# A Linformer attention with a gated FFN: PSUM banks of the first batch laid out by hand, two head groups reordered, and the second batch's K projected apart from V

## The chip, the cores and the metric

The kernel runs on one core of a Trainium2 chip. The core has five engines with instruction streams of their own: TensorE (PE, the matmuls), VectorE (DVE), ScalarE (ACT), GpSimd (POOL) and SyncE (SP). Here POOL and SP mostly start DMA transfers. PE writes its results into eight PSUM banks of 128 partitions by 512 fp32 values; ACT and DVE read them there. The metric is the time of one execution on the device, in microseconds; the number given is the median of several runs.

## The reference

Eight batches, eight heads, 1024 positions, 64 values per head. K and V are first projected along the sequence from 1024 rows to 64 (E and F), so that the softmax of each position runs over 64 scores only. The heads are put side by side to rows of 512, and these go through a gated feed-forward layer with 1536 hidden values.

```python
k_proj = np.einsum('ks,bhsd->bhkd', E, k)          # (8, 8, 64, 64)
v_proj = np.einsum('ks,bhsd->bhkd', F, v)
scores = np.matmul(q, k_proj.transpose(0, 1, 3, 2)) / np.sqrt(64)
attn = softmax(scores)                             # over the 64 projected rows
x = np.matmul(attn, v_proj)                        # then to (8 * 1024, 512)
gate = 1.0 / (1.0 + np.exp(-(x @ w_gate)))
out = (gate * (x @ w_val)) @ w_out                 # w_gate, w_val: 512 x 1536, w_out: 1536 x 512
```

## The kernel before

**How the order is made.** Every operation is handed to a planner (`Plan.add`, L38) with the engine, what it reads and writes and the PSUM bank that it uses. Each engine runs its operations in the order in which they were handed over; the planner only adds semaphore waits where an operation depends on one of another engine. A bank is one such resource (`x=[("bank", b)]` in `mm`, `act` and `dve`, L202 to L218): a matmul into a bank waits for whoever read the bank last, and a reader waits for the reader before it, on whatever engine. So an operation that waits holds up all that was handed over to its engine behind it. There is no other scheduling: the order of the calls is the order of the work.

**Banks.** Four banks are called pF0 to pF3 (`FB`), four pA0 to pA3 (`AB`). A `Ring` (L191) gives them out in turn. `whole` (L200) turns over pA0 to pA3 and pF0 to pF2, `ffn` over the four F banks, `att` over the four A banks. Each call of `next()` takes the next one, whether it is free or not.

**First batch (L951 to L998).** All data come from HBM, so the start is a chain: E and F are transposed (`project_consts`, L413); `project` (L447) multiplies K's four heads by E; `keep_k` copies the product out, `turn_k` (L487) transposes it back on PE, and ACT writes `kpD`. In `half_unit` (L513) come, for one half of each position block and one group R of four heads: `qt` (PE transposes Q, two engines copy it to `qT`), `sc` (scores, then exponentials to `eT` on ACT), `den` (sums of the exponentials; DVE makes the reciprocal `rden` and splits it into two bf16 parts, `rhi` and `rhl`), `bc` (PE spreads the reciprocals over the partitions, ACT copies them to `rb`), and `xo` (attention times V; DVE multiplies by `rb` into `xT`). V is projected by `v_part` (L972) and copied to `vpD` by `keep_v` on ACT and DVE. `busy(n)` (L437) puts n matmuls of the identity by itself into pF3, whose result nobody reads. `first_pair` (L877) then begins the feed-forward layer with two of its column blocks at once, with `xo` of the second head group in between.

**The main loop (L1007 to L1060).** For each batch b it makes a list `todo` of steps: two halves (blk) of 12 steps `mstep` (L870: four matmuls for the gate, four for the value, 128x512 each, then `gate`: the sigmoid as a tanh on ACT to `sig`, and the product on DVE to `hT`), and output projections `oproj` (L923: 12 matmuls, a copy on DVE, a DMA by SP) in between. The step uses two F banks, so that step m + 2 needs the banks of step m. `put(i, fn)` hangs a piece of the attention of the next batch behind entry i of the list; `spots` (L1038, L1040) holds these places. For the first batch the entries are 0 to 10 (first half; entry 0 is the pair of the steps 0 and 1), 11 to 22 (steps 0 to 11 of the second half) and 23 to 26 (four `oproj`).

**The second batch's attention** (`attention(1)`, L666) differs from the later ones. `kv` (L669) projects K and V into one bank, 32 matmuls, and copies K once and V four times, all on ACT; `turn_kd` transposes K on PE; `den` makes four reciprocals, `split` the bf16 parts; `bc` spreads by matmuls. Batches from the third on use DMA transposes and POOL for these steps. `sc` and `xo` take four banks of `att` each.

POOL issues all loads in program order: those of the first batch, of Q(1), K(1), V(1) and w_out (which waits for the transposes of Q(1)), then of the batches after. K(1) lies in buffer KV2, which V(2) is loaded into later. SP issues the DMA transposes of Q(1), four transfers, and the stores.

Of the kernel before, what the change touches and what calls it, by code (L numbers as in the profile page):

```python
# [8 lines left out]
BF16 = mybir.dt.bfloat16  # L9
# [109 lines left out]
def bass_linformer_attn__then__ffn_glu_sigmoid_kernel(  # L119
# [18 lines left out]
    with contextlib.ExitStack() as es:  # L138
# [58 lines left out]
                self.turn += 1  # L197
                return b

        whole, ffn, att = Ring(AB + FB[:3]), Ring(FB), Ring(AB)  # L200

        def mm(b, o, lhsT, rhs, r, start=True, stop=True, tp=None, tr=False):  # L202
            kw = {}
# [8 lines left out]
        def act(o, i, r, w, b=None, func=AF.Copy, scale=1.0):  # L212
            x = [] if b is None else [("bank", b)]
            return add("ACT", lambda e: e.activation(o, i, func, scale=scale), r=r, w=w, x=x)  # L214

        def dve(fn, r, w, b=None):
            x = [] if b is None else [("bank", b)]
            return add("DVE", fn, r=r, w=w, x=x)  # L218
# [294 lines left out]
        def half_unit(hf, ring):  # L513
# [2 lines left out]
            qv = qT[s][:, :, :].rearrange("p (R x) c -> p R x c", R=2)  # L516

            def qt(R, engines):
                bk = ring.next()
                ob = bank[bk][:, :].bitcast(BF16)  # L520
                for x in range(4):
                    for t in range(2):
                        c = x * 2 + t
                        mm(
                            bk,
                            ob[:, c * P : (c + 1) * P],
                            Qb[s][:, 4 * R + x, (2 * hf + t) * P : (2 * hf + t + 1) * P],
                            ident[:, :],
                            [("Q", s, hf, R), "ident"],
                            tr=True,  # L530
                        )
                o = qv[:, R, :, 256 * hf : 256 * hf + 256]
                i = ob[:, :].rearrange("p (x c) -> p x c", x=4)
                for rr, eng in enumerate(engines):
                    oo, ii = (a[:, 2 * rr : 2 * rr + 2, :] for a in (o, i))
                    ws = [("qT", s, hf, R, rr)]
                    if eng == "ACT":
                        act(oo, ii, [], ws, b=bk)
                    else:
                        dve(lambda e, oo=oo, ii=ii: e.tensor_copy(oo, ii), [], ws, b=bk)  # L540

            def sc(R):
                bks = [ring.next(), ring.next()]
# [122 lines left out]
        def attention(b):  # L666
            s = b % 2

            def kv():  # L669
                bk = att.next()  # L670
                if b == 1:
                    project(2 * b % 3, 0, [bk, bk], 0)
                    project((2 * b + 1) % 3, 1, [bk, bk], 256)
                    keep_k(bk, 0)
                    keep_v([bk, bk], 256, ["ACT"] * 4)
                    return
                for t in range(NT):
                    for w in range(2):
                        n = (2 * b + w) % 3
                        src = KV[n][:, :, :].rearrange("p h (t d) -> p t h d", t=NT)  # L680
                        mm(
                            bk,
                            bank[bk][64 * w : 64 * w + 64, :],
                            EFT[:, t, 64 * w : 64 * w + 64],
                            src[:, t, :, :],
                            [("KV", n, 0), ("KV", n, 1), ("EFT", t // 4)],
                            start=(t == 0),
                            stop=(t == NT - 1),
                            tp=(0, 64 * w),
                        )  # L690
                act(
                    kpd[:, :, :, :],
                    bank[bk][0:64, :]
                    .rearrange("p (h d) -> p h d", h=H)
                    .unsqueeze(2)
                    .to_broadcast([64, H, 2, DH]),
                    [],
                    ["kpd"],
                    b=bk,
                )  # L700
                for g in range(2):
                    act(
                        vpD[64 * g : 64 * g + 64, :, :].rearrange("p h d -> p (h d)"),
                        bank[bk][64:128, :],
                        [],
                        [("vpD", h, g, R) for h in range(2) for R in range(2)],
                        b=bk,
                    )

            def turn_kd():  # L710
                if b == 1:
                    turn_k(att)
                    return
                add(
                    "SP",
                    lambda e: e.dma_start_transpose(
                        kpD[:, :, :],
                        kpd[:, :, :, :].rearrange("p h g d -> p (h g d)"),
                    ),
                    r=["kpd"],  # L720
                    w=[("kpD", 0), ("kpD", 1)],
                    dma="kpD",
                )
# [98 lines left out]
            def xo(r2):  # L822
                for r in (2 * r2, 2 * r2 + 1):
# [13 lines left out]
                    for g in range(2):  # L837
# [10 lines left out]
                            b=bks[g],  # L848
                        )

            return [
                kv,
                turn_kd,
                lambda: sc(0),
                lambda: sc(1),
                den,
                split if b == 1 else gather,
                (lambda: bc(0)) if b == 1 else (lambda: spread(0)),
                (lambda: bc(1)) if b == 1 else (lambda: spread(1)),
                lambda: xo(0),  # L860
                lambda: xo(1),
            ]
# [88 lines left out]
        start_loads()  # L951
        constants()
        project_consts()
        busy(40)
        qt, sc, den, bc, xo = half_unit(0, whole)
        for R in range(2):
            bk = whole.next()
            project(0, 0, [bk, bk], 0, R)
            busy(4)
            keep_k(bk, 0, R)  # L960
            turn_k(whole, R)
            busy(8)
        qt(0, ("DVE", "ACT"))
        busy(6)
        sc(0)
        qt(1, ("DVE", "DVE"))
        busy(6)
        den(0)
        sc(1)
        busy(4)  # L970

        def v_part(R, ring):  # L972
            bks = [ring.next(), ring.next()]
            project(1, 1, bks, 0, R)
            keep_v(bks, 0, ["ACT", "DVE", "ACT", "DVE"], R)

        bc(0)
        den(1)
        v_part(0, whole)
        busy(4)  # L980
        bc(1)
        xo(0)
        busy(8)
        for _ in range(-att.turn % 4):
            att.next()
        v_part(1, att)
        start_xo = half_unit(0, att)[4]
        load_q(1)
        load_k(1)
        load_v(1)  # L990
# [16 lines left out]
        for b in range(B):  # L1007
            todo = []
            for blk in (2 * b, 2 * b + 1):
                ms = [[m] for m in range(NF)]  # L1010
                if blk == 0:
                    ms = [[0, 1]] + ms[2:]
                if blk == 1:
                    gaps = {11: [0, 1, 2, 3]}
                else:
                    gaps = {2: [0], 5: [1], 8: [2], 11: [3]}
                for m in ms:
                    if len(m) == 2:
                        todo.append(lambda: first_pair(lambda: start_xo(1)))
                    else:  # L1020
                        todo.append(lambda blk=blk, m=m[0]: mstep(blk, m))
                    if blk >= 1:
                        for tt in gaps.get(m[-1], ()):
                            todo.append(lambda blk=blk, tt=tt: oproj(blk - 1, tt, ffn.next()))
            at = {}

            def put(i, fn):
                at.setdefault(i, []).append(fn)

            if b == 0:  # L1030
                qt, sc, den, bc, xo = half_unit(1, att)
                put(5, lambda: (qt(0, ("DVE", "ACT")), qt(1, ("DVE", "ACT"))))
                put(6, lambda: sc(0))
                put(7, lambda: (den(0), sc(1)))
                put(8, lambda: (den(1), bc(0)))
                put(9, lambda: (xo(0), bc(1)))
                put(10, lambda: xo(1))
                spots = (16, 17, 18, 19, 20, 20, 22, 23, 24, 25)  # L1038
            else:
                spots = (3, 6, 10, 13, 16, 16, 20, 23, 26, 29)  # L1040
            if b + 1 < B:
                for i, fn in zip(spots, attention(b + 1)):
                    put(i, fn)
            def load_next(n):
                load_k(n)
                load_q(n)
                load_v(n)

            if b == 0:
                put(17, lambda: load_next(2))  # L1050
                put(25, lambda: transpose_q(2))
            else:
                if b + 2 < B:
                    put(4, lambda b=b: load_next(b + 2))
                    put(20, lambda b=b: transpose_q(b + 2))
            for i, slot in enumerate(todo):
                slot()
                for fn in at.get(i, ()):
                    fn()
            assert max(at, default=0) < len(todo)  # L1060
        last = 2 * B - 1
        for tt in range(4):
            oproj(last, tt, whole.next())

        plan.emit(nc, es, final=[f"out{i}" for i in range(4)])

# [27 lines left out]
```

The softmax here doesn't subtract the row's maximum and nothing guards it: scores larger than these inputs give would overflow.

## Time and profile before

| what | value | where from |
|---|---|---|
| median of 3 runs | 576.91 us (576.17 to 576.95) | the runs |
| the profiled execution | 575.25 us | its own time |
| its span | 573.4 us | the profile |
| PE standing, 10.97 to 20.00 us | 9.03 - 7.25 = 1.78 us | busy time by stretches |
| PE standing, 20.00 to 28.80 us | 8.80 - 5.91 = 2.89 us | the same |
| PE standing, 28.80 to 53.70 us | 24.90 - 23.72 = 1.18 us | the same |
| PE standing, 69.60 to 80.46 us | 10.86 - 9.05 = 1.81 us | the same |
| PE standing, 80.46 to 559.70 us | 0.00 us | the same |
| granted PE clock | 1.00 in every stretch | the same |

The span is the time from the first to the last instruction of the profiled execution; that execution's own time is 1.85 us longer, and the median of the other runs 1.66 us longer again. Times inside the execution are counted from the span's start. A line of the timeline holds the start, the duration from the first to the last of a merged group, the engine, the line of the kernel, the operation with output and input, the number of instructions, and in square brackets how long the engine had been idle and what ended it. "PEld" is the loading of weights, which overlaps the matmuls.

When transfers of the first two batches were issued and landed (issue + time to landing, from the answers on the tiles):

| load | issued | landed |
|---|---|---|
| K(0), first and second half of the heads | 1.34, 2.24 | 9.3, 12.0 |
| Q(0), first and second half of the heads | 2.98, 3.73 | 13.4, 14.7 |
| V(0), first and second half of the heads | 4.44, 5.2 | 18.4, 20.9 |
| w_gate and w_val, chunk 3 (steps 6 and 7) | 13.34, 14.07 | 33.0, 34.3 |
| K(1), V(1) | 18.6, 19.5 | 50.1, 56.7 |

### The profile page before, as it was taken

The numbers are of one execution on the slowest core, as the hardware profiler recorded it, in microseconds if no ns is written. First come the engines' busy times: TensorE is split into PE (matmuls) and PEld (weight loads), VectorE is DVE, ScalarE is ACT, GpSimd is POOL, SyncE is SP. The second block draws the span as 40 slices with busy tenths as digits, with TensorE's granted clock in tenths as the row PEclk, the third lists the DMA queues.
The fourth block names the chain that finished last, engine by engine and source line by source line (L and its number), as shares of the span: only waits on it lengthen the run. The fifth ranks groups of instructions, "written<-read, shape, count | busy, mean of one in ns | idle before, by whom it ended". The sixth has DMA issues, their size and how long they took to land.

```text
span 573.4 us, 7766 instructions
## 1 busy us (share of the span) xinstructions
PE 556.9 (97%) x3060; PEld 248.8 (43%) x3060; DVE 251.5 (44%) x403; ACT 176.2 (31%) x310; POOL 107.2 (19%) x148
## 2 busy tenths in 40 slices
PE   5799989999999999999999999999999999999997
PEld 5443434444444444444444444444444444444443
DVE  3546356325633546335453264434463354633332
ACT  2444561342224322333223422144223332222220
POOL 9400200104400071001800035000610007000000
PEclk9999999999999999999999999999999999999999
DMA  9999896955656159430796046670501101010012
GB/s 159 199 201 186 144 204 159 173 112 104 113 117 102 37 113 153 86 84 22 123 170 116 23 85 107 138 105 37 113 19 46 38 20 39 37 38 21 35 38 91
DMA packets 76421, 56.02 MB, mean 98 GB/s; under 512 B 34688, under 2 KB 67968, under 8 KB 76384
## 3 DMA queue, kind: packets, MB, share of 16 engines
q0 software_dynamic: 33984, 29.89, 34.4%
q1 hardware_dynamic: 42400, 25.63, 17.6%
q8 instruction: 24, 0.39, 0.3%
q14 instruction: 13, 0.11, 0.1%
HBM read 60.29 MB, written 16.78 MB: 134 GB/s over the span
## 4 chain that ended last, share of the span: by engine, by line
PE 95%; DVE 3%; ACT 1%; issue 0%; DVEq 0%
PE pF L210 86%; PE pA L210 9%; ACT eT L214 1%; DVE rden L769 1%; DVE xT L639 0%; DVE rden L583 0%; DVE count L327 0%; DVE hT L910 0%; DVE dsel L388 0%; ACT sig L214 0%; DVE rhl L780 0%; DVE rhl L594 0%; DVE ost L937 0%; ACT qT L214 0%; ACT kp L214 0%
## 5 line engine op out<-in xcount | busy, mean ns | idle before, releaser
L910 DVE SCALAR_TENSOR_TENSOR hT<-sig,pF 128x512 bf16<-128x512 f32 x192 | 130.7, 685 | 200.5 <-PE pF L210 153.1
L214 ACT ACTIVATE sig<-pF 128x512 f32<-128x512 f32 x192 | 114.3, 599 | 317.6 <-PE pF L210 315.2
L210 PE MATMUL pF<-xT,wG 128*128 128x512 bf16 x768 | 198.3, 379 | 1.8 <-DVE xT L639 1.8
L210 PE MATMUL pF<-xT,wV 128*128 128x512 bf16 x768 | 197.7, 379 | 0.0
L210 PE MATMUL pF<-wO,hT 128*128 128x512 bf16 x732 | 168.1, 379 | 0.0
L210 PEld LDWEIGHTS pF<-xT,wV 128*128 128x128 bf16 x768 | 75.2, 98 | 90.3
L210 PEld LDWEIGHTS pF<-xT,wG 128*128 128x128 bf16 x768 | 72.2, 98 | 96.6 <-issue 12.9
L815 POOL PARTITION_BROADCAST rb<-rrow x96 | 70.7, 798 | 217.1 <-DMA rrow<-rden 212.0
L210 PEld LDWEIGHTS pF<-wO,hT 128*128 128x128 bf16 x732 | 70.4, 98 | 88.7 <-issue 6.2
L937 DVE TENSOR_SCALAR ost<-pF 128x512 f32<-128x512 f32 x61 | 42.2, 692 | 97.8 <-PE pF L210 95.5
L214 ACT ACTIVATE eT<-pA 128x512 bf16<-128x512 f32 x62 | 32.2, 606 | 9.5 <-PE pA L210 9.5
L840 DVE TENSOR_TENSOR xT<-pA,rb 128x512 bf16<-128x512 f32 x56 | 34.7, 682 | 0.0
L228 POOL DMA_DIRECT2D KV<-in_v_dram x9 | 7.8, 871 | 87.3 <-PE pF L210 84.9
L769 DVE RECIPROCAL rden<-pA 128x128 f32<-128x128 f32 x28 | 23.7, 909 | 0.0
L210 PE MATMUL pA<-KV,EFT 128*64 128x512 bf16 (+2 forms) x176 | 15.4, 319 | 1.0 <-DVE xT L639 1.0
L214 ACT ACTIVATE kpd<-pA 64x1024 bf16<-64x1024 f32 x6 | 6.1, 1017 | 28.3 <-PE pA L210 28.3
L228 POOL DMA_DIRECT2D KV<-in_k_dram x9 | 8.0, 890 | 33.3 <-PE pF L210 33.2
L210 PEld LDWEIGHTS pA<-KV,EFT 128*64 128x64 bf16 x176 | 8.0, 109 | 8.0 <-issue 4.1
L210 PE MATMUL pA<-qT,kpD 64*64 64x512 bf16 (+1 forms) x136 | 10.2, 370 | 0.5 <-ACT qT L214 0.3
L210 PE MATMUL pA<-eT,vpD 64*64 64x512 bf16 (+1 forms) x140 | 10.4, 367 | 0.0
L214 ACT ACTIVATE vpD<-pA 64x512 bf16<-64x512 f32 (+2 forms) x20 | 9.7, 484 | 2.2 <-PE pA L210 1.8
L228 POOL DMA_DIRECT2D Qb<-in_q_dram x11 | 9.4, 866 | 0.0
(70 smaller groups left out, 109.3 us busy)
## 6 DMA issues: line engine op xcount, KB each, us to landing
out_dram<-ost SPq DMA_DIRECT2D x64, 256.0 KB, 2.0
Qb<-in_q_dram POOLq DMA_DIRECT2D x7, 1024.0 KB, 15.9
KV<-in_k_dram POOLq DMA_DIRECT2D x7, 1024.0 KB, 10.8
KV<-in_v_dram POOLq DMA_DIRECT2D x7, 1024.0 KB, 11.4
wO<-in_moe_w_out_dram POOLq DMA_DIRECT2D x1, 1536.0 KB, 13.0
wG<-in_moe_w_gate_dram POOLq DMA_DIRECT2D x5, 256.0 KB, 19.7
wV<-in_moe_w_val_dram POOLq DMA_DIRECT2D x5, 256.0 KB, 20.2
KV<-in_k_dram POOLq DMA_DIRECT2D x2, 512.0 KB, 8.9
```

The costliest lines, as they stand in the source:

```text
L210: return add("PE", lambda e: e.matmul(o, lhsT, rhs, **kw), r=r, x=[("bank", b)])
L214: return add("ACT", lambda e: e.activation(o, i, func, scale=scale), r=r, w=w, x=x)
L228: add("POOL", lambda e: e.dma_start(o, i), r=r, w=w, dma=sem)
L769: lambda e, cc=cc: e.reciprocal(rden[:, cc], bank[bk][:, cc]),
L815: lambda e, n=n, i=2 * rnd + c, j=j, parts=parts: e.partition_broadcast(rb[0:parts, n, :], rrow[32 * j : 32 * j + 1, i, :], channels=parts),
L840: lambda e, r=r, g=g, n=n, bk=bks[g]: e.tensor_tensor(xT[s][:, r, :, 256 * g : 256 * g + 256], bank[bk][:, :].rearrange("p (f c) -> p f c" ...
L910: lambda e: e.scalar_tensor_tensor(hT[blk % 2][:, m, :], sg[:, :], 1.0, bank[pv][:, :], ALU.add, ALU.mult,),
L937: lambda e: e.tensor_scalar(o[:, :], bank[pb][:, :], 0.5, None, op0=ALU.mult),
```

## The change

- `whole` becomes a list of 28 banks in an order written by hand, one entry for each bank that the first half of the first batch takes; `v_part(1)` and the `xo(1)` in `first_pair`, which took banks of `att`, now take them from it, and the last four `oproj` take F banks.
- `qt` takes a bank for each of its two copies, with four transposes each, where one bank held all eight; this holds for both halves of the first batch. In the list, the two banks of `qt(1)` are the same one, pA3.
- In the first half, `sc(1)` goes ahead of `den(0)`, and `den(1)` ahead of `bc(0)`. The fillers change from 40 to 20 at the start, from 8 to 10 behind the first K projection and to 4 behind the second, and by some more from `sc(1)` on.
- For the second batch, `kv` is split into `k_alone` and `v_alone`, each with a bank of `att`. The spots become 13 (K), 14 (its transposes), 16 (V and `sc(0)`), 17 (`sc(1)`), 18 (`den` and `split`), 21 and 23 (`bc`), 24 and 25 (`xo`); they were 16 (K and V), 17, 18, 19, 20 (`den` and `split`), 22, 23, 24, 25.

```diff
--- before.py
+++ after.py
@@ -197,7 +197,24 @@
                 self.turn += 1
                 return b
 
-        whole, ffn, att = Ring(AB + FB[:3]), Ring(FB), Ring(AB)
+        A0, A1, A2, A3 = AB
+        F0, F1, F2, F3 = FB
+        whole = Ring(
+            (A0, A1)
+            + (A2, A3, F0, F1)
+            + (A0, A1)
+            + (F2, A2)
+            + (A3, A3)
+            + (F0, F1)
+            + (A0, A1)
+            + (A2, A0)
+            + (A3, F0)
+            + (F1, F2)
+            + (A1, A2)
+            + (A3, A0)
+            + (A1, A2)
+        )
+        ffn, att = Ring(FB), Ring(AB)
 
         def mm(b, o, lhsT, rhs, r, start=True, stop=True, tp=None, tr=False):
             kw = {}
@@ -516,28 +533,27 @@
             qv = qT[s][:, :, :].rearrange("p (R x) c -> p R x c", R=2)
 
             def qt(R, engines):
-                bk = ring.next()
-                ob = bank[bk][:, :].bitcast(BF16)
-                for x in range(4):
-                    for t in range(2):
-                        c = x * 2 + t
-                        mm(
-                            bk,
-                            ob[:, c * P : (c + 1) * P],
-                            Qb[s][:, 4 * R + x, (2 * hf + t) * P : (2 * hf + t + 1) * P],
-                            ident[:, :],
-                            [("Q", s, hf, R), "ident"],
-                            tr=True,
-                        )
-                o = qv[:, R, :, 256 * hf : 256 * hf + 256]
-                i = ob[:, :].rearrange("p (x c) -> p x c", x=4)
                 for rr, eng in enumerate(engines):
-                    oo, ii = (a[:, 2 * rr : 2 * rr + 2, :] for a in (o, i))
+                    bk = ring.next()
+                    ob = bank[bk][:, :].bitcast(BF16)
+                    for x in range(2):
+                        for t in range(2):
+                            c = x * 2 + t
+                            mm(
+                                bk,
+                                ob[:, c * P : (c + 1) * P],
+                                Qb[s][:, 4 * R + 2 * rr + x, (2 * hf + t) * P : (2 * hf + t + 1) * P],
+                                ident[:, :],
+                                [("Q", s, hf, R), "ident"],
+                                tr=True,
+                            )
+                    o = qv[:, R, 2 * rr : 2 * rr + 2, 256 * hf : 256 * hf + 256]
+                    i = ob[:, 0:512].rearrange("p (x c) -> p x c", x=2)
                     ws = [("qT", s, hf, R, rr)]
                     if eng == "ACT":
-                        act(oo, ii, [], ws, b=bk)
+                        act(o, i, [], ws, b=bk)
                     else:
-                        dve(lambda e, oo=oo, ii=ii: e.tensor_copy(oo, ii), [], ws, b=bk)
+                        dve(lambda e, o=o, i=i: e.tensor_copy(o, i), [], ws, b=bk)
 
             def sc(R):
                 bks = [ring.next(), ring.next()]
@@ -668,12 +684,6 @@
 
             def kv():
                 bk = att.next()
-                if b == 1:
-                    project(2 * b % 3, 0, [bk, bk], 0)
-                    project((2 * b + 1) % 3, 1, [bk, bk], 256)
-                    keep_k(bk, 0)
-                    keep_v([bk, bk], 256, ["ACT"] * 4)
-                    return
                 for t in range(NT):
                     for w in range(2):
                         n = (2 * b + w) % 3
@@ -707,10 +717,17 @@
                         b=bk,
                     )
 
+            def k_alone():
+                bk = att.next()
+                project(2 * b % 3, 0, [bk, bk], 0)
+                keep_k(bk, 0)
+
+            def v_alone():
+                bk = att.next()
+                project((2 * b + 1) % 3, 1, [bk, bk], 0)
+                keep_v([bk, bk], 0, ["ACT"] * 4)
+
             def turn_kd():
-                if b == 1:
-                    turn_k(att)
-                    return
                 add(
                     "SP",
                     lambda e: e.dma_start_transpose(
@@ -848,15 +865,29 @@
                             b=bks[g],
                         )
 
+            if b == 1:
+                return [
+                    k_alone,
+                    lambda: turn_k(att),
+                    v_alone,
+                    lambda: sc(0),
+                    lambda: sc(1),
+                    den,
+                    split,
+                    lambda: bc(0),
+                    lambda: bc(1),
+                    lambda: xo(0),
+                    lambda: xo(1),
+                ]
             return [
                 kv,
                 turn_kd,
                 lambda: sc(0),
                 lambda: sc(1),
                 den,
-                split if b == 1 else gather,
-                (lambda: bc(0)) if b == 1 else (lambda: spread(0)),
-                (lambda: bc(1)) if b == 1 else (lambda: spread(1)),
+                gather,
+                lambda: spread(0),
+                lambda: spread(1),
                 lambda: xo(0),
                 lambda: xo(1),
             ]
@@ -951,7 +982,7 @@
         start_loads()
         constants()
         project_consts()
-        busy(40)
+        busy(20)
         qt, sc, den, bc, xo = half_unit(0, whole)
         for R in range(2):
             bk = whole.next()
@@ -959,32 +990,30 @@
             busy(4)
             keep_k(bk, 0, R)
             turn_k(whole, R)
-            busy(8)
+            busy(10 if R == 0 else 4)
+
+        def v_part(R):
+            bks = [whole.next(), whole.next()]
+            project(1, 1, bks, 0, R)
+            return lambda: keep_v(bks, 0, ["ACT", "DVE", "ACT", "DVE"], R)
+
         qt(0, ("DVE", "ACT"))
         busy(6)
         sc(0)
         qt(1, ("DVE", "DVE"))
         busy(6)
+        sc(1)
         den(0)
-        sc(1)
-        busy(4)
-
-        def v_part(R, ring):
-            bks = [ring.next(), ring.next()]
-            project(1, 1, bks, 0, R)
-            keep_v(bks, 0, ["ACT", "DVE", "ACT", "DVE"], R)
-
+        busy(10)
+        den(1)
         bc(0)
-        den(1)
-        v_part(0, whole)
-        busy(4)
+        v_part(0)()
+        busy(6)
         bc(1)
         xo(0)
-        busy(8)
-        for _ in range(-att.turn % 4):
-            att.next()
-        v_part(1, att)
-        start_xo = half_unit(0, att)[4]
+        busy(4)
+        keep = v_part(1)
+        keep()
         load_q(1)
         load_k(1)
         load_v(1)
@@ -1016,7 +1045,7 @@
                     gaps = {2: [0], 5: [1], 8: [2], 11: [3]}
                 for m in ms:
                     if len(m) == 2:
-                        todo.append(lambda: first_pair(lambda: start_xo(1)))
+                        todo.append(lambda: first_pair(lambda: xo(1)))
                     else:
                         todo.append(lambda blk=blk, m=m[0]: mstep(blk, m))
                     if blk >= 1:
@@ -1028,14 +1057,14 @@
                 at.setdefault(i, []).append(fn)
 
             if b == 0:
-                qt, sc, den, bc, xo = half_unit(1, att)
-                put(5, lambda: (qt(0, ("DVE", "ACT")), qt(1, ("DVE", "ACT"))))
-                put(6, lambda: sc(0))
-                put(7, lambda: (den(0), sc(1)))
-                put(8, lambda: (den(1), bc(0)))
-                put(9, lambda: (xo(0), bc(1)))
-                put(10, lambda: xo(1))
-                spots = (16, 17, 18, 19, 20, 20, 22, 23, 24, 25)
+                qt2, sc2, den2, bc2, xo2 = half_unit(1, att)
+                put(5, lambda: (qt2(0, ("DVE", "ACT")), qt2(1, ("DVE", "ACT"))))
+                put(6, lambda: sc2(0))
+                put(7, lambda: (den2(0), sc2(1)))
+                put(8, lambda: (den2(1), bc2(0)))
+                put(9, lambda: (xo2(0), bc2(1)))
+                put(10, lambda: xo2(1))
+                spots = (13, 14, 16, 16, 17, 18, 18, 21, 23, 24, 25)
             else:
                 spots = (3, 6, 10, 13, 16, 16, 20, 23, 26, 29)
             if b + 1 < B:
@@ -1060,7 +1089,7 @@
             assert max(at, default=0) < len(todo)
         last = 2 * B - 1
         for tt in range(4):
-            oproj(last, tt, whole.next())
+            oproj(last, tt, ffn.next())
 
         plan.emit(nc, es, final=[f"out{i}" for i in range(4)])
```

## The prediction

> **What bounds the kernel now.** I read the busy shares first: TensorE (PE) is busy for 97% of the span, so a change pays only where PE stands still, and costs where it makes PE stand still. The chain of waits says where. From 93 us to 559.7 us it is PE alone, piece after piece as below; no edit to the first two batches is worth anything in there.
>
> ```profile
> PE 556.9 (97%) x3060; PEld 248.8 (43%) x3060; DVE 251.5 (44%) x403; ACT 176.2 (31%) x310; POOL 107.2 (19%) x148
> ```
> ```profile
> 28.82 10.52 PE pF L210 x48
> ...
> 170.12 13.06 PE pF L210 x60
> ```
>
> The table by stretches gives PE's standing time: 1.78 us in 10.97 to 20.00, 2.89 us in 20.00 to 28.80, 1.18 us in 28.80 to 53.70, 1.81 us in 69.60 to 80.46, nothing between 80.46 and 559.70. The change works on the first, second and fourth. In order of time, the start (start, duration, engine, line, what, the wait before it):
>
> ```profile
> 7.28 3.76 PE L210 MATMUL pF<-ident 128*128 128x128 bf16 x40
> 10.97 0.64 PE L210 MATMUL pA<-KV,EFT 128*64 128x128 bf16 x16
> 15.80 0.60 ACT L214 ACTIVATE qT<-pF 128x512 bf16<-128x512 bf16 x1 [1.03 <-DVE qT L540]
> 25.28 0.64 PE L210 MATMUL pA<-KV,EFT 128*64 128x128 bf16 x16 [1.02 <-DVE xT L639]
> 28.82 0.59 PE L210 MATMUL pF<-xT,wG 128*128 128x512 bf16 x2 [0.63 <-DVE xT L639]
> ```
>
> Fillers to 10.97, an ACT copy that waits for a DVE copy of the same bank, a V projection that waits for a bank, and at 28.82 the gapless stream. The second batch's attention stands like this:
>
> ```profile
> 66.03 1.57 ACT L214 ACTIVATE vpD<-pA 64x256 bf16<-64x256 f32 x4
> 69.62 0.63 PE L210 MATMUL pA<-qT,kpD 64*64 64x512 bf16 x8
> 70.13 2.06 ACT L214 ACTIVATE eT<-pA 128x512 bf16<-128x512 f32 x4 [0.60 <-PE pA L210]
> 75.77 3.38 DVE L769 RECIPROCAL rden<-pA 128x128 f32<-128x128 f32 x4
> 80.32 1.28 DVE L910 SCALAR_TENSOR_TENSOR hT<-sig,pF 128x512 bf16<-128x512 f32 x2
> 80.46 0.40 PE L210 MATMUL pA<-rhl,bsel 32*128 32x512 bf16 x4 [1.82 <-DVE rhl L780]
> ```
>
> Its one stall: `bc(0)` waits for `rhl`, behind four reciprocals.
>
> **The start, step by step.** *Fillers 40 to 20.* They start at 7.28. 12 of them lie in 9.10 to 10.10 and 13 in 10.30 to 10.80, half as long: the pace doubles near 10.25. The first 28 take about 0.107 us each, so 20 end at 7.28 + 2.14 = 9.42. K's first half, issued at 1.34, landed 8.0 us later (9.34), so its projection moves from 10.97 to 9.42. But the second half, issued at 2.24, landed after 9.8 us, at 12.04:
>
> ```profile
> DMA to landing us min/median/max: 8.0/8.9/9.8
> ```
>
> The first half's projection (1.0 at the slow pace), `kp` (0.28), its transposes (0.30) and 10 fillers (0.55) with hand-overs end near 11.7 and hide in that landing. The second projection goes from 12.88 to 12.06: of 1.55 us, 0.82 is left; the landing takes the rest. *Fillers 8 to 4 behind it*: 4 x 0.055 = 0.22; `qt(0)` from 14.69 to 13.65, after Q's landing (2.98 + 10.4 = 13.38).
>
> *A bank for each `qt` copy.* ACT's copy started 0.46 after DVE's, for the bank alone. Now both have their own: the second half of `sc(0)`, 16.45, comes 1.04 + 0.46 = 1.50 earlier, 14.95, its exponentials at 15.35. `qt(1)` is the odd one: both parts are put into bank A3, so its second four transposes wait for the first DVE copy. Start 15.18, first copy 15.61 to 16.03 (0.43 behind four transposes, 0.42 long), second transposes 16.08, second copy 16.51 to 16.93. It costs 0.4 against one fill, yet is over before the 18.10 of now.
>
> *`sc(1)` before `den(0)`.* `sc(1)` ends up at 16.98 instead of 18.31, its exponentials at 17.38 to 18.46. `den(0)` stands behind it, at 17.21; its reciprocal, 0.57 behind the start, goes from 18.42 to 17.78 and `rhl(0)` (0.96 + 0.28 + 0.35 with gaps) from 20.06 to 19.42. `den(1)` no longer stands behind `bc(0)`: it runs at 18.5, and its reciprocal follows `rhl(0)` on DVE, 19.44 instead of 21.01, so `rhl(1)` is ready at 21.05 instead of 22.62. The V copies queued behind end at 21.58 (now 23.16), `xo(0)` goes from 23.30 to 21.72, and `xT` of it from 25.14 to 23.56. V's halves landed at 18.44 and 20.9 and hold nothing.
>
> *`v_part(1)`.* It waited 1.02 for A0 and then took 0.57 ahead of the first MLP matmuls. Its new banks A3 and A0 are free by 21.6, so it runs at 22.1 in the shadow of `xT`. The first MLP matmul goes from 25.85 to 23.70; `xo(1)` from 26.82 to 24.66, its `xT` to 26.52, the gapless stream from 28.82 to 26.66. **Start: -2.16 us.** The weights have room: the tightest, chunk 3, issued at 13.34 and 14.07, landed at 33.0 and 34.3, needed at 35.1 and 36.0 (37.25 and 38.1 less 2.16). Bounds: 1.4 gained if the slow pace lasts 0.8 us of work longer (next but one paragraph), 2.6 if every hand-over of 0.1 to 0.15 on this chain shrinks.
>
> The second half of the first batch uses two banks more for `qt`, but PE runs through it; its one stall (52 to 53.7, `xT`) stays. The last four `oproj` on the F banks find them read long before: 0.
>
> A rule speaks against this edit. The Trainium skill ("TensorE: Matmul & The Clock Gate", Part 1) says that PE runs at half clock until a free-running window of about 3.4 us has been busy. Halving the fillers, by that rule, risks the release slipping one window to about 13.7; as an estimate by the page that would make the start -1.4 instead of -2.16. The row shows the halving of the pace, but not what releases it. The sum goes without this: in the new order PE has work without a break until 10.3, past the 10.25 of now. The price of a later release comes from rows: projection, transposes and fillers from 12.06 on at twice their 0.57, 0.30 and 0.22, some 0.8 us.
>
> **The second batch.** *K apart from V*: the 32 matmuls of 1.87 us become 16 and 16, 0.94 each: 0. K lands at 50.1, V at 56.7, PE asks at 56.7 and 63.0: hidden. POOL's load of V(2), which waited 2.43 us for K's buffer, starts up to 2.4 us earlier, needed at 100.8: 0. SP loses nothing; its transposes of Q end by 60.2, and `sc(0)` asks at 64.
>
> *`v_alone` with `sc(0)` directly behind.* The att ring stands at turn 18 when the batch begins (4 + 2 + 3 + 3 + 4 + 2), so K has A2, its transposes A3, V has A0, and `sc(0)` A1, A2, A3, **A0**. The fourth bank is the one that ACT is still emptying. Counting from the start of `v_alone`, T: last V matmul at 0.98, the four ACT copies 1.17 to 2.74 (1.57, the row above), while PE has done five of the eight `sc(0)` matmuls (0.07 each) by 1.39. PE waits until 2.79: **1.40 us new stall**, bounds 1.2 (copies start as soon as the matmuls end) and 1.6. Before, a whole MLP step and the transposes of K lay between. Behind that wait stand all of PE's stream; late next are the exponentials, 2.74 to 4.80, `sig`, and those of `sc(1)`, 5.40 to 7.52.
>
> *`den` and `split` after step 7, `bc(0)` after step 10.* Now three MLP steps (5.19 us) cover the 6.0 us from `den` to `rhl`, where two did. But `hT` of step 8 stands behind the reciprocals and the split on DVE, and step 10 needs its bank (four F banks, two to a step). From the end of the exponentials to the first reciprocal took 75.77 - 74.65 = 1.12; so reciprocals at 8.64 to 12.02, `hT` 8 ends 12.02 + 1.17 + 0.69 = 13.88. Step 8 starts 0.37 behind the exponentials, 7.89; V of step 10 would start 4.33 later, 12.22, and starts at 13.93: **1.71 us stall**, in the place of the 1.88 at `bc(0)`, which then finds `rhl` ready. Bounds 1.3 and 2.1 by how soon `sig` 7 gets through ACT. In the base the two steps behind `den` asked for no bank still held. **Batch: +1.40 + 0.07 (`den` waits for the last exponential) + 1.71 - 1.88 = +1.30 us**, between 0.9 and 1.9.
>
> **Sum.** -2.16 + 1.30 = -0.86 us. The profiled execution took 575.25 with a span of 573.4, so it would be about 574.4; against the median of the runs, 576.91, it is 576.05. About 0.2% (1.15 us) is what a measurement of this kernel can tell from no change; -0.86 is inside. The bounds give -2.6 + 0.9 = -1.7 to -1.4 + 1.9 = +0.5, so 575.2 to 577.4 for this case alone.
>
> **Rivals.**
> 1. *The new waits of the second batch are cheaper.* If the wait on A0 isn't there (ACT done in time, or a ring order I miscounted), the sum is -0.86 - 1.40 = -2.26: 574.65. For it: 1.6 us of copies is a short work. Against: ring and program order leave PE nothing else to do. 0.25, all faster.
> 2. *Slower: the pace stays halved through the start.* Place: from 12.06 to the gapless stream. PE streams on the chain there (projection, transposes, `sc`, `den`, `bc`, `xo`, the eight first MLP matmuls) sum to 0.57 + 0.30 + 0.22 + 0.45 + 0.22 + 0.34 + 0.34 + 0.34 + 0.34 + 1.73 = 4.9 us, and would take as much again. It decides where more than 2.0 of these 4.9 are lost (then +1.15 with the batch); all lost give 576.05 + 4.9 = 581. A typical case, half of it, 578.5. For it: 74 fillers in place of 92. Against: PE stood 2.89 us of 8.8 in 20 to 28.8 and kept its pace. 0.17.
> 3. *The change doesn't do what it says*: the start is set by landings (12.04, 13.38, 14.75) that come late in other executions, so only 0.8 us is gained there; 576.91 - 0.8 + 1.3 = 577.4. For it: two of the three are met within 0.4 us. Against: they are met, not waited for long. 0.13, mostly no change.
>
> **From these the numbers.** The forecast has 0.45: a third of it is faster by over 0.2%. Faster 0.15 + 0.25 = 0.40; within 0.2% 0.30 + 0.10 = 0.40; slower 0.17 + 0.03 = 0.20. Time 576.0. The range runs from 574.4, just below rival 1, to 577.9, past rival 3 and into rival 2.
>
> **What the new profile must show.** K's first projection near 9.4 and the second at 12.0 to 12.1; no wait of ACT's `qT` on DVE; no wait ahead of the V projection near 22; the gapless stream from 26.4 to 27.0. In the second batch, PE waiting about 1.4 us for ACT `vpD` inside `sc(0)`, about 1.7 us for DVE `hT` inside step 10, and none at `bc(0)`. The forecast is wrong if either wait is missing, if fillers or projections after 10.3 still run 0.1 us apart, or if a wait turns up between 93 and 559.7 us of now.

## The result and the profile after

The changed kernel takes 575.17 us (median of 4 runs, 574.51 to 575.20); before, 576.91 (576.17 to 576.95). The ratio is 0.997 with a 95% interval of 0.9953 to 0.9987: 1.74 us faster, forecast 0.86. Yet the profiled executions of the two took the same time, 575.20 and 575.25 us, both with a span of 573.4. So the medians and the profiles disagree; why they do became the main finding.

Busy time by stretches of the changed kernel (length, PE, weight loads, DVE, ACT, POOL, clock, DMA share, GB/s), to be set against the table of before:

```profile
10.97:20.00 9.03, 7.46 (x116) 5.19 (x114) 3.14 (x6) 4.00 (x9) 9.03 (x13) 1.00 1.33 201
20.00:28.80 8.80, 6.72 (x88) 3.69 (x90) 5.49 (x13) 3.72 (x9) 0.50 (x1) 1.00 1.45 196
...
53.70:69.60 15.90, 14.64 (x104) 6.69 (x105) 4.62 (x7) 8.40 (x17) 3.65 (x4) 1.00 0.97 145
69.60:80.46 10.86, 9.26 (x50) 3.69 (x50) 7.25 (x11) 5.33 (x11) 0.00 (x0) 1.00 1.23 202
```

PE stands 0.81 us less from 20.00 to 28.80, but 1.26 us between 53.70 and 69.60, where it had stood for next to nothing in the kernel before:

```profile
53.70:69.60 15.90, 15.89 (x102) 7.75 (x102) 4.81 (x7) 7.04 (x14) 3.66 (x4) 1.00 0.95 134
```

The timeline of the start of the changed kernel:

```profile
7.48 2.34 PE L227 MATMUL pF<-ident 128*128 128x128 bf16 x20
12.30 0.64 PE L227 MATMUL pF<-KV,EFT 128*64 128x128 bf16 x16
14.54 0.60 ACT L231 ACTIVATE qT<-pA 128x512 bf16<-128x512 bf16 x1 [0.35 <-PE pA L227]
19.05 0.63 DVE L605 CAST rhi<-rden 64x128 bf16<-64x128 f32 x1
20.11 0.40 PE L227 MATMUL pA<-rhl,bsel 32*128 32x128 bf16 x8 [0.92 <-DVE rhl L610]
27.31 0.59 PE L227 MATMUL pF<-xT,wG 128*128 128x512 bf16 x2 [0.62 <-DVE xT L655]
```

ACT's copy no longer waits for DVE, and the gapless stream begins at 27.31, 1.51 us earlier than the 28.82 of before. But `bc(0)` starts at 20.11, exactly as before: a DVE copy that took 0.27 us took 0.63. In the kernel before it stood here:

```profile
19.40 0.27 DVE L589 CAST rhi<-rden 64x128 bf16<-64x128 f32 x1
```

The second batch of the changed kernel:

```profile
64.92 1.58 ACT L231 ACTIVATE vpD<-pA 64x256 bf16<-64x256 f32 x4 [1.23 <-PE pA L227]
66.55 0.41 PE L227 MATMUL pA<-qT,kpD 64*64 64x512 bf16 x3 [1.16 <-ACT vpD L231]
72.42 3.38 DVE L786 RECIPROCAL rden<-pA 128x128 f32<-128x128 f32 x4
76.97 1.28 DVE L941 SCALAR_TENSOR_TENSOR hT<-sig,pF 128x512 bf16<-128x512 f32 x2
77.71 1.04 PE L227 MATMUL pF<-xT,wV 128*128 128x512 bf16 x4 [1.55 <-DVE hT L941]
78.68 0.40 PE L227 MATMUL pA<-rhl,bsel 32*128 32x512 bf16 x4
```

Both new waits are there, and `bc(0)` finds its input ready. The idle time in brackets counts from the end of the last matmul; the time lost to issue is some 0.2 more each. At the start of `xo(1)`, the last piece of that attention (89.76 before, 89.70 now), 0.06 us of the 1.51 is left: the second batch gave back 1.45.

### The profile page after: what moved, and what is told of

Same layout as the page of the kernel before. It is cut to its first block, busy times and chain, and to the rows that moved or that the text cites. A ratio compares the mean times of both kernels' runs of the same rounds, so it can differ in the third digit from the quotient of the medians.

```text
span 573.4 us, 7674 instructions
## 1 busy us (share of the span) xinstructions
PE 552.7 (96%) x2987; PEld 247.8 (43%) x3042; DVE 252.0 (44%) x403; ACT 176.5 (31%) x310; POOL 107.2 (19%) x148
## 4 chain that ended last, share of the span: by engine, by line
PE 95%; DVE 2%; issue 1%; DMA 1%; ACT 0%; SPq 0%; DVEq 0%
PE pF L227 87%; PE pA L227 7%; DMA EF<-in_F_dram 1%; DVE rden L786 1%; DVE xT L655 0%; DVE hT L941 0%; DVE rden L599 0%; ACT vpD L231 0%; DVE rhi L605 0%; DVE vpD L502 0%; DVE rhl L610 0%; DVE ost L968 0%; ACT qT L231 0%; SPq L314 0%; DVE rhi L795 0%
## 5 line engine op out<-in xcount | busy, mean ns | idle before, releaser
L227 PE MATMUL pF<-xT,wG 128*128 128x512 bf16 x748 | 194.8, 380 | 3.4 <-DVE xT L655 1.8
L227 PE MATMUL pF<-wO,hT 128*128 128x512 bf16 x750 | 173.9, 379 | 1.5 <-issue 0.8
L227 PEld LDWEIGHTS pF<-wO,hT 128*128 128x128 bf16 x768 | 74.0, 98 | 93.0 <-issue 6.0
L968 DVE TENSOR_SCALAR ost<-pF 128x512 f32<-128x512 f32 x64 | 44.3, 692 | 103.0 <-PE pF L227 103.0
L231 ACT ACTIVATE rb<-pA 128x512 f32<-128x512 f32 x14 | 7.4, 599 | 8.1 <-PE pA L227 8.1
```

The lines of the kernel that those rows point to most:

```text
L227: return add("PE", lambda e: e.matmul(o, lhsT, rhs, **kw), r=r, x=[("bank", b)])
L968: lambda e: e.tensor_scalar(o[:, :], bank[pb][:, :], 0.5, None, op0=ALU.mult),
```

## The experiments

Medians, and ratios to the kernel before as measured beside each (576.84 to 576.88 us). The intervals are 0.7 to 1.1 us to either side, so where two of these kernels differ by less than that, the trace has to carry the reading:

| kernel | us | ratio, 95% interval |
|---|---|---|
| before_again (unchanged) | 576.55 | 1.000, 0.9987 to 1.0012 |
| start_only | 573.76 | 0.9960, 0.9945 to 0.9975 |
| batch_only | 578.40 | 1.0032, 1.0017 to 1.0046 |
| v_one_step_earlier | 573.85 | 0.9959, 0.9945 to 0.9974 |
| before_gaps_filled | 575.26 | 0.9979, 0.9967 to 0.9992 |
| after_gaps_bare | 576.61 | 1.0005, 0.9993 to 1.0017 |
| after_loads_held | 574.62 | 0.9963, 0.9950 to 0.9975 |
| after_40_fillers | 576.06 | 0.9989, 0.9976 to 1.0002 |
| held_shifted | 573.34 | 0.9944, 0.9927 to 0.9961 |
| held_shifted_spread | 571.22 | 0.9912, 0.9893 to 0.9931 |

**before_again.** No edit.

> The kernel before, unchanged, profiled once more. Its first profiled execution took 575.25 us, below every timed run of it (576.17 to 576.95). Theory: that execution was an early one, and a usual one has its gapless stream begin about 1.5 us later than 28.82 us; then this profile shows a later start. Rival: the start is the same in all executions and the difference lies in the stream behind 93 us; then the stream begins at 28.8 again and the end is later for the same start. Time 576.9 against itself, ratio 1.000.

This profiled execution took 578.04 us, with a span of 576.2. Stretches of its start, PE's busy time and clock (the first two columns behind the length, and the number ahead of the DMA share):

```profile
17.81:21.22 3.41, 1.86 (x33) 1.00 1.39 195
21.22:24.63 3.41, 3.10 (x50) 0.51 1.45 196
24.63:28.04 3.41, 2.84 (x34) 0.50 1.45 195
28.04:31.45 3.41, 3.41 (x16) 0.50 1.45 196
```

The granted clock falls to one half at 21.28 us and comes back at 31.52; the stream at full pace begins at 31.6, not 28.8, 2.8 us later where the theory had 1.5. The theory's "later start" holds, with a cause that the first profile did not contain: that one had clock 1.00 throughout. In the 3.41 us ahead of the fall PE is busy for 1.86. The longest gap in it is a wait for `rhl`, 1.53 us where the first profile had 1.06. The difference is the copy `rhi` ahead of it, 0.75 us in place of 0.27:

```profile
19.82 0.75 DVE L589 CAST rhi<-rden 64x128 bf16<-64x128 f32 x1
21.01 0.22 PE L210 MATMUL pF<-rhl,bsel 32*128 32x128 bf16 x1 [1.53 <-DVE rhl L594]
```

**start_only** and **batch_only.** Each half of the change alone; in the first, `kv` and the spots are those of before, in the second all that lies ahead of the main loop.

```diff
-                spots = (13, 14, 16, 16, 17, 18, 18, 21, 23, 24, 25)
+                spots = (16, 17, 18, 19, 20, 20, 22, 23, 24, 25)
```

> The new first batch with the second batch of before. Theory (two parts that add): the gapless stream begins at 27.3 as in the changed kernel, the second batch stalls 1.9 us at bc(0) and nowhere else, so about 1.3 us faster than the changed kernel: 573.9, 3.0 us below before. Rival (the whole gain sits in the second batch or elsewhere): no faster than the changed kernel, 575.2 or above.

> The first batch of before with the new second batch. Theory: waits of 1.2 to 1.4 us in sc(0) for ACT's vpD and of 1.5 to 1.7 in step 10 for DVE's hT, in the place of 1.9 at bc(0): 1.2 to 1.4 us slower than before, 578.2. Rival (the split of K and V pays by itself, through earlier loads or shorter waits): same as before or faster, 576.9 or less.

Both times are as the first theory has them: 573.76 and 578.40. The new second batch costs 575.17 - 573.76 = 1.41 us behind the new start and 578.40 - 576.84 = 1.56 behind the old one; its waits in batch_only are 1.16 and 1.55 us again. Within the intervals the parts add. One thing was not as expected: in the profile of start_only, whose first batch is that of the changed kernel, the gapless stream begins at 26.65, not at 27.3. There the pace of PE doubled earlier, the second half of K set the second projection (11.99, behind a wait of 0.41 for the transfer), and `rhi` took 0.22 us:

```profile
26.65 0.59 PE L227 MATMUL pF<-xT,wG 128*128 128x512 bf16 x2 [0.62 <-DVE xT L655]
```

That execution took 573.08 us, one of the short ones of its six (573.00 to 574.52); the changed kernel's profile, at 575.20, was one of its long ones. So the start of the stream differs by 0.66 us between executions of the same first batch.

**v_one_step_earlier.**

```diff
-                spots = (13, 14, 16, 16, 17, 18, 18, 21, 23, 24, 25)
+                spots = (13, 14, 15, 16, 17, 18, 18, 21, 23, 24, 25)
```

> The changed kernel with v_alone behind entry 15 of the list in place of 16, so that one MLP step lies between ACT's copies and sc(0). Theory: the wait in sc(0) (1.16 us in its trace) is gone, the wait in step 10 stays: 1.1 to 1.4 us faster than the changed kernel, 573.9. Rival (the wait only moves to the next one, ACT being the bound between sc(0) and den): less than 0.4 us faster, 574.8 to 575.2.

573.85, 1.32 below the changed kernel; of the two waits only the 1.55 us for `hT` is left in its trace. One MLP step between ACT's copies and the scores takes away the whole first wait.

**before_gaps_filled** and **after_gaps_bare.** Fillers alone, put into the kernel before (the diff) or taken out of the changed one (`busy(6)`, `busy(6)`, `busy(10)`, `busy(6)` and `busy(4)` from `qt(0)` on).

```diff
         sc(1)
-        busy(4)
+        busy(22)
...
         v_part(0, whole)
-        busy(4)
+        busy(18)
...
         xo(0)
-        busy(8)
+        busy(24)
```

> The kernel before, with 22, 18 and 24 fillers where it has 4, 4 and 8 (behind sc(1), v_part(0) and xo(0)), enough at 0.055 us each to fill PE's three gaps between 19 and 25 us and too few to run past them; nothing else. Theory (in most executions of the kernel before, PE's clock falls to one half for 7 to 10 us from 21 to 22 us on, because of these gaps): the clock stays at 1.00, the gapless stream begins at 28.8 or before, all executions lie at 575.0 to 575.6, 1.3 to 1.6 us below the kernel before. Rival (the clock falls for another reason, or the gain of the changed kernel comes from its order alone): no change, 576.3 to 577.0, with the same spread.

> The changed kernel without its 32 fillers between qt(0) and v_part(1) (6, 6, 10, 6 and 4); the fillers ahead of that stay. Theory (the gaps make the clock fall): the clock is at one half for 7 or 10 us somewhere between 17 and 32 us and the time is 576 to 578, with a wider spread. Rival (the fillers do nothing, the order sets the time): 574.9 to 575.3, as the changed kernel, clock 1.00 throughout.

Same stretches of three profiles, first before_again, then before_gaps_filled, then after_gaps_bare:

```profile
20.00:28.80 8.80, 6.91 (x79) 4.37 (x80) 4.84 (x11) 3.61 (x9) 0.53 (x1) 0.57 1.45 195
```
```profile
20.00:28.80 8.80, 7.52 (x115) 4.86 (x111) 5.20 (x11) 3.06 (x9) 0.50 (x1) 1.00 1.45 196
```
```profile
20.00:28.80 8.80, 6.67 (x70) 3.54 (x72) 5.52 (x13) 3.16 (x8) 0.50 (x1) 0.50 1.45 195
```

Busy time hardly tells the first from the third; the clock does. With its gaps filled, the kernel before runs at 575.26, ten of twelve runs between 574.55 and 575.46, and all twelve keep the clock (a mean of 0.999 or 1.000 over the execution). Of the 35 runs of the plain one beside it 25 lost it for a time (mean 0.991 or 0.994) and took 576.06 to 578.19; of the ten that kept it, five lay at 575.24 to 575.39 and five at 576.09 to 576.28. The changed kernel without its late fillers runs at 576.61 and lost the clock in all twelve runs (mean 0.988 to 0.994); the wider spread that was expected did not come, eleven of the twelve lie within 0.52 us.

So most of the measured gain is the clock, not the order. Over the 64 runs of the kernel before that stand beside the experiments, the median is 576.92 us for the 43 that lost the clock and 575.39 for the 21 that kept it. Every profiled execution with the new start and its fillers kept it; among the timed runs with that start a few show a mean of 0.996 or 0.997 (one of six in start_only and in v_one_step_earlier, three of twelve in after_40_fillers). At equal clock the change is worth 575.39 - 575.17 = 0.22 us by these medians, 575.26 - 575.17 = 0.09 against the kernel with its gaps filled, and 0.05 by the two first profiles: nothing that these runs can tell from zero. What makes some runs at full clock 0.8 us longer than others (576.1 in place of 575.3) is not shown; no profile of the kernel before fell on one of them.

**after_loads_held.**

```diff
-        load_q(1)
+        load_q(1, [("rhl", 1)])
```

> The changed kernel with POOL's loads of Q(1), K(1) and V(1) waiting for rhl(1), so that POOL issues no transfer while DVE copies rden to rhi. Theory (the first rhi copy, 0.63 us in the changed kernel's profile against 0.22 for the second, is held by POOL's issue of a load and ends with it at 19.7): rhi takes 0.22 to 0.28 and bc(0) starts 0.3 to 0.4 earlier, 574.8. The transfers land up to 3.3 us later and are still early enough. Rival (the long copy is something else, or the chain has slack there): rhi stays at 0.4 to 0.7, or the time at 575.2.

574.62, 0.55 below the changed kernel, and all twelve runs (574.00 to 574.80) lie below three of the changed kernel's four (575.17 to 575.20); the intervals of the two overlap. `bc(0)` starts at 19.51 and the stream at 26.71. DVE and POOL in the changed kernel, then in this one:

```profile
18.60 1.03 POOL L245 DMA_DIRECT2D KV<-in_k_dram  x1
19.05 0.63 DVE L605 CAST rhi<-rden 64x128 bf16<-64x128 f32 x1
```
```profile
18.86 0.22 DVE L606 CAST rhi<-rden 64x128 bf16<-64x128 f32 x1
19.11 0.34 DVE L611 SCALAR_TENSOR_TENSOR rhl<-rhi,rows,rden 64x128 bf16<-64x128 bf16 x1
...
21.38 0.89 POOL L245 DMA_DIRECT2D Qb<-in_q_dram  x1 [3.52 <-DVE vpD L503]
```

The copy ended at 19.68, 0.05 behind POOL's issue of the load (18.60 + 1.03); with POOL quiet it takes 0.22. That the loads have to be held for this is not shown by the one profile, since start_only's has the short copy with POOL's loads in place; what the twelve runs show is that none is as long as 575.2. The held loads landed hardly later (K(1) at 49.4 against 48.9), probably because the transfers ahead of them set that.

**after_40_fillers.**

```diff
-        busy(20)
+        busy(40)
```

> The changed kernel with 40 fillers at the start, as before, in place of 20. Theory (20 fillers let K's first projection start when its data land, and what they lose in pace is less): K's second projection at 12.7 to 13.0 in place of 12.0 to 12.5, the stream 0.5 later, 575.7. Rival (the fillers at the start set when the clock is released, and the 20 pay for it as much as they save): the same time, 575.2.

576.06, 0.89 slower by the medians: the theory, with a bigger size. The runs lie in three groups from 575.16 to 576.82, the first as short as the changed kernel's, and the two intervals overlap, so the time alone does not settle it. In the profile K's second projection starts at 13.11 in place of 12.30, and the long `rhi` copy (0.69) now ends with POOL's next load at 20.54, so that `bc(0)` starts at 20.98.

**held_shifted** and **held_shifted_spread.** The loads held, and the second batch's places moved; in the second also one reciprocal to a step.

```diff
-                spots = (13, 14, 16, 16, 17, 18, 18, 21, 23, 24, 25)
+                spots = (12, 13, 14, 15, 16, 17, 17, 22, 23, 24, 25)
...
-                    split,
+                    lambda: recip(1),
+                    lambda: recip(2),
+                    lambda: (recip(3), split()),
...
-                spots = (12, 13, 14, 15, 16, 17, 17, 22, 23, 24, 25)
+                spots = (12, 13, 14, 15, 16, 17, 18, 19, 20, 22, 23, 24, 25)
```

> The changed kernel with the three loads held, and the second batch's places at 12 (K), 13 (its transposes), 14 (V), 15 and 16 (sc), 17 (den and split), 22, 23 (bc), 24, 25 (xo): a step between V and sc(0), and four steps between den and bc(0). Theory: of the two waits the one in sc(0) is gone (1.2 us) and the one for DVE's hT stays (1.55 us, now in step 9), since reciprocals and split still stand in a row on DVE: 573.4. Rival (with more steps between den and bc(0) the second wait goes too): 571.9.

> The same with den's four reciprocals one by one behind entries 17, 18, 19 and 20, the split with the last, so that each hT on DVE waits for one reciprocal at most. Theory (the second wait is hT standing behind the row of reciprocals): it goes, no wait in the second batch, 571.9, 1.5 below the run with the row. Rival (DVE is short of time there in any order): the wait only moves to bc(0) or a later step, 573.0 to 573.4.

573.34 and 571.22. The first keeps one wait in the second batch:

```profile
73.84 1.04 PE L227 MATMUL pF<-xT,wV 128*128 128x512 bf16 x4 [1.55 <-DVE hT L942]
```

In the second PE is busy all through:

```profile
53.70:80.46 26.76, 26.76 (x172) 11.58 (x170) 12.82 (x18) 15.58 (x31) 3.65 (x4) 1.00 1.07 170
```

The row of reciprocals, not a lack of DVE time, made that wait: DVE is busy for 12.82 of 26.76 us. It is the best version: 5.66 us below the kernel before measured beside it, 3.95 below the changed one.

## Why the prediction was right or wrong

**The sum** gave 576.05 and the runs 575.17: the direction, and inside the range. But it is right as a total of errors of opposite sign, not step by step: the start gained 0.65 us less in the trace and the second batch cost 0.15 more, which leaves -0.06 of the -0.86, and against that stand some 1.7 us, most of them the clock, that the sum did not contain. That the total came so near is luck.

**The start, forecast -2.16, in the trace -1.51.** Most steps came as described: K's first projection early, ACT's `qT` free of DVE, the second V projection without its 1.02 us wait, no wait on a bank but A3's. Up to the first reciprocal 0.28 of the loss arose: PE began 0.20 later in this execution, behind the landing of F, and the fillers' pace doubled near 11.6 in place of 10.1 to 10.25. So PE's own slow work set K's second projection, at 12.30, and not the landing, as the sum had it (12.06): in this execution the second half of K had landed at 2.24 + 8.7 = 10.9. The rest, 0.35, is one mis-sized term: `rhl(0)` "0.96 + 0.28 + 0.35" took the 0.28 of `rhi` from a row where the copy fell at the end of POOL's issue. Moved earlier, it ran into that issue and took 0.63. `bc(0)` and all behind it kept the sum of both, 0.65.

Neither loss comes in every execution. In start_only's profile, with the same first batch, the second projection does wait for the landing, `rhi` takes 0.22, and the stream begins at 26.65, where the sum had 26.66. By the medians, start_only against the kernel before with its gaps filled, the start is worth 575.26 - 573.76 = 1.50 us. So the chain was right, and the sum priced one of its shorter executions.

**The second batch, forecast +1.30, in the trace +1.45, in the runs +1.41.** This is the part that held best: the wait on A0 (1.40 forecast; 1.16 by the idle time, 1.42 from the sixth score matmul's turn at 65.13 to 66.55), the wait for `hT` of step 8 (1.71; 1.55 by idle time, 1.72 from 75.99 to 77.71), and nothing at `bc(0)`. v_one_step_earlier took the first away and got 1.3 us, held_shifted_spread the second and got 2.1 against held_shifted; the last figure is above the 1.55 of the wait, and of the difference 0.25 us lies in an earlier start of the stream in its profile (26.31 against 26.56).

**What failed.** Under the second rival stands "PE stood 2.89 us of 8.8 in 20 to 28.8 and kept its pace". This came from one execution, and that one, at 575.25 us, was faster than every timed run shown (576.17 to 576.95): it was one of the third of all executions that keep their clock (25 of the 76 measured later). The text set the sum against its time and passed over what the difference to the median might hold. I looked for the clock as a danger to the new order; it was the trouble of the old one, and most of the gain is the end of it. The rival itself, that the new order would run at half pace, did not come; after_gaps_bare shows that it would have without the late fillers.

**The rivals.** The first, cheaper waits in the second batch, fell: its time of 574.65 was near, for the wrong reason. The third, a start set by the landings, explains 0.2 of the 0.65 us at most.

The fillers at the start were probably halved rightly: with 40 the kernel is 0.89 us slower by the medians. The doubling of the pace came 1.5 us later in the changed kernel's profile; but in start_only, with the same 20, K's first projection already ran at full pace at 9.49. By the clock record of the twelve traces the moment lies between 8.51 and 11.04 us in the five profiles with 40 fillers and between 8.46 and 11.63 in the seven with 20, so it differs between executions and these runs do not show that the fillers move it. The slip to about 13.7 that the prediction held possible is in none of them.

## What to carry to other kernels

Look at whether the profiled execution's time lies among the timed runs before it is used as the base of a sum; if it lies outside, something in it is not as usual, and the granted clock by stretches is the first place to look. Price an edit in a start phase also by the gaps that it leaves PE, since a gap can cost its own length and then several microseconds at half clock; dummy matmuls in gaps where PE waits anyway cost nothing that these runs can measure (575.26 with them, 575.24 to 575.39 in the short runs without). A consumer placed directly behind the copies that free its buffer, and a row of long operations ahead of short ones on an in-order engine, each show as one wait whose size follows from the row's length: put a step between, or deal the row out one to a step.

## What the runs showed of the hardware

- **The clock falls without a long gap.** Half clock lasted 10.24 us in before_again (21.28 to 31.52), 6.83 in batch_only (22.16 to 28.99) and 13.65 in after_gaps_bare (17.78 to 31.43): 3, 2 and 4 times 3.413 us. Each fall, too, comes a whole number of such lengths behind the moment at which the pace first doubled (11.04, 8.51 and 10.95): 3, 4 and 2 of them. The Trainium skill ("TensorE: Matmul & The Clock Gate", Part 1) states a free-running window of 3413 ns, which these lengths bear out. The advice of the same page ("Why this matters for your kernels") against idle gaps of over about 3 us does not cover this case, where the longest gap ahead of the fall in before_again was 1.53 us. The measurement decides: shorter gaps can be enough.
- **PE's busy time does not tell which window loses the clock.** In the last 3.41 us ahead of the three falls PE was busy for 1.86, 1.89 and 2.23 us. The windows at the start of the first profile of the kernel before, counted from 10.12, where its pace doubled, held 2.33 and 2.25 us (16.95 to 20.36 and 20.36 to 23.77), and the clock stayed. But it also stayed through a later window of the same count, the line below, in which PE was busy for less than in any of the others, with the wait of 1.82 us at `bc(0)` in it. What else counts is not shown; the matmuls of that window are larger (128x512) than most of those ahead of the falls, but no run varied that. What is shown is the remedy: with fillers in its gaps the kernel before kept the clock in twelve of twelve runs, and without them the changed kernel lost it in twelve of twelve.

```profile
78.39:81.80 3.41, 1.59 (x11) 1.00 1.24 207
```

- **A DVE copy from SBUF to SBUF can be held by POOL's issue of a load.** `rhi` took 0.63, 0.75, 0.71 and 0.69 us (the changed kernel, before_again, after_gaps_bare, after_40_fillers) where it began 0.31 to 0.45 us behind the start of an issue, and ended 0.04 to 0.05 us behind the end of that issue each time; with POOL quiet it took 0.22. The Trainium skill ("SBUF — State Buffer", Who interferes with whom) describes a port pair that DVE's faster copies and GpSimd share as an exclusive lock. The common ends agree with that; that it is this lock, no run here shows. Not every overlap holds the copy: begun 0.05 to 0.14 us behind the issue's start (batch_only, 18.69 and 18.64; start_only, 18.73 and 18.64; before_gaps_filled, 18.75 and 18.61) it took 0.22.
